# A linear-attention layer and a gated convolution unit: keys and values two tokens to a row, 64-row matmul tiles, a compact state and a new order of the work

## The chip, the cores and the metric

The kernel runs on one core of a Trainium2 chip. The core has a matrix engine (TensorE, PE in the profile; its weight loads are PEld), a vector engine (VectorE, DVE), a scalar engine (ScalarE, ACT), a general one (GpSimd, POOL) and a queue engine (SyncE, SP) that mostly issues DMAs. The matrix engine writes its results into PSUM, eight banks of 512 fp32 columns on 128 partitions; VectorE and ScalarE read them from there. The engines run side by side and wait for one another by semaphores. The metric is the device time of one execution in microseconds, here the median of several runs.

## The reference

Inputs are r, k and v of shape (4 batches, 8 heads, 768 tokens, 48 channels), decays w and bonuses u of shape (8, 48), and three weights of the second layer. All are fp32.

```python
state = zeros((B, H, D, D))
for t in range(S):
    cur = einsum('bhd,bhe->bhde', u * k[t], v[t])
    y[t] = einsum('bhd,bhde->bhe', r[t], state + cur)
    state = w[:, :, None] * state + einsum('bhd,bhe->bhde', k[t], v[t])
x = y.transpose(0, 2, 1, 3).reshape(B, S, H * D)        # 384 channels
gate = sigmoid(sum(conv_w[i] * shifted(x, 4 - i) for i in range(5)))   # causal, per channel
out = (gate * (x @ w_val)) @ w_out
```

The recurrence need not be run token by token. Within a chunk, y is a masked product of scores (r times k, with the decays folded into both) and v, plus r times the state at the chunk's start, plus the bonus of the token itself.

## The kernel before, in words

A unit is 256 tokens of one batch; there are 12 units, three to a batch, and each has two chunks of 128 tokens. For each unit the stages are, by the names of the order that is written out in the code:

- **r, k, v** load the inputs. r comes with two neighbouring tokens of a head to a partition row (`load_r`, 384 bytes in a piece), k and v with one token to a row (`load_kv`, 192 bytes in a piece), a chunk at a time.
- **RS, KS** multiply r and k by tables of decays (`scale_r` L245, `scale_k` L274; POOL, some on DVE). **RT, KT** transpose them on PE, eight 128x128 transposes each (L259, L297). **RE, KE** copy the transposes from PSUM on ACT (`evac_r` L267, which also brings r's two tokens of a row back into the order of time, and `evac_k` L307). **CV** casts v to bf16 (L283, ACT).
- **PR, S, SE, DV** make the bonus: r times k (L316, DVE), a sum over channels by matmuls with two columns (L328), its copy (L340), and v times it (L343, POOL).
- **A** makes the scores of a chunk, eight matmuls with 48 rows and 128 columns into two banks (L357); **M** masks one bank of them on DVE (L370), four to a unit.
- **KV, ID, ZE** keep the state. A matmul for two heads at a time gives a 96x96 block of which only the two 48x48 blocks on the diagonal count (L384); DVE adds the old state in PSUM (L396) and multiplies by a mask of 384 columns that also holds the decay (L401).
- **YD, Y** put y together in a bank for each chunk: the bonus by six matmuls with the identity (L412), the state's and the scores' part by matmuls of 128 rows and 32 columns (`mm`, L426), 28 to a chunk. **YE** copies it to xT, channels on partitions (L455, ACT).
- **C, SG, V, HT, O, OE, st** are the second layer: the convolution as matmuls with diagonal 64x64 blocks (`conv` L470, 40 to a unit), the sigmoid (L483, ACT), the value matmuls (L490 and L499), their product with the gate (L512, DVE), the projection (L522), its copy (L534, ACT) and the store. The last unit is done a chunk at a time (`conv_l`, `value_l` and so on).

Nothing plans this at run time. The string `ORDER` (L639) lists all stages of all units, and each engine gets its instructions in that order; `r:1*` with a star means the other queue or engine. So an instruction that waits holds back all that follows it on its engine. SP issues nearly all DMAs in that order too. The matrix engine's banks come from a pool of eight that hands out the next one (`bank`, L58).

Ahead of the units stand the tables: w is loaded, its log taken (LN), and four exponentials give the decays (DRI, DKI). `dummy` (D, L146) is three matmuls of 512 columns that compute nothing.

Of the kernel before, what the change touches and what calls it, by code (L numbers as in the profile page):

```python
# [12 lines left out]
AX = mybir.AxisListType  # L13
# [3 lines left out]
def kernel(  # L17
# [21 lines left out]
    U = 2  # L39
    W = U * C  # L40
    NU = S // W
    N = B * NU
# [3 lines left out]
    ld = ctx.enter_context(tc.tile_pool(name="ld", bufs=7))  # L46
    ldr = ctx.enter_context(tc.tile_pool(name="ldr", bufs=6))
    wk = ctx.enter_context(tc.tile_pool(name="wk", bufs=2))
    atp = ctx.enter_context(tc.tile_pool(name="atp", bufs=4))
    ffn = ctx.enter_context(tc.tile_pool(name="ffn", bufs=2))  # L50
    outp = ctx.enter_context(tc.tile_pool(name="outp", bufs=11))

    psum = ctx.enter_context(tc.tile_pool(name="psum", bufs=8, space=bass.MemoryType.PSUM))
# [4 lines left out]
    def bank(shape=(128, 512), dtype=F32):  # L58
        return psum.tile(list(shape), dtype, name="bank")

    k_st, v_st, r_st = {}, {}, {}

    def load_kv(n, cl, nm, eng):
        b, cu = divmod(n, NU)
        src, d = (k, k_st) if nm == "k" else (v, v_st)
        if n not in d:
            d[n] = ld.tile([128, U, H, D], F32, name=f"{nm}_st")
        t0 = cu * W + cl * C
        eng.dma_start(out=d[n][:, cl], in_=src[b, :, t0 : t0 + C, :].transpose([1, 0, 2]))

    def load_r(n, eng, hs=(0, H)):
        b, cu = divmod(n, NU)
        if n not in r_st:
            r_st[n] = ldr.tile([128, H, 2, D], F32, name="r_st")
        hs = slice(*hs)
        eng.dma_start(
            out=r_st[n][:, hs].rearrange("p h s d -> p h (s d)"),
            in_=r[b, hs, cu * W : cu * W + W, :].rearrange("h (p s) d -> p h (s d)", s=2),
        )

    w_bc = consts.tile([128, H, D], F32)
    cw5 = consts.tile([KW, DM], F32)

    def load_w():
        nc.sync.dma_start(
            out=w_bc.rearrange("p h d -> p (h d)"),
            in_=w.rearrange("(o h) d -> o (h d)", o=1).to_broadcast([128, DM]),
        )

    def load_cw():  # L90
        nc.sync.dma_start(out=cw5, in_=moe_conv_w)
# [3 lines left out]
    wt = consts.tile([128, NP], F32)  # L95
    nc.vector.memset(wt, 1.0)
    ut = consts.tile([128, NP], F32)
    nc.vector.memset(ut, 0.0)
    nc.scalar.preload_act_table_set("natural_log_exp_and_others")
    for dst, src in ((wt, w), (ut, u)):  # L100
        for par in range(2):
            nc.scalar.dma_start(
                out=dst[64 * par : 64 * par + D, :],
                in_=src.rearrange("(p two) d -> two d p", two=2)[par],
            )


    io_i32 = consts.tile([128, 1], mybir.dt.int32)
    nc.gpsimd.iota(io_i32, pattern=[[0, 1]], base=0, channel_multiplier=1)
    io_j = consts.tile([128, 2], mybir.dt.int32)  # L110
    nc.gpsimd.iota(io_j, pattern=[[1, 2]], base=0, channel_multiplier=2)
    mask = consts.tile([128, 128], BF16)
    make_upper_triangular(nc, mask, val=1.0, diag=False)

    io_f = consts.tile([128, 1], F32)
    nc.vector.tensor_copy(io_f, io_i32)
    sc_k = consts.tile([128, U], F32)
    for cl in range(U):
        nc.vector.tensor_scalar(
            sc_k[:, cl : cl + 1], io_f, scalar1=-1.0, scalar2=float(C - 1 - cl * C),  # L120
            op0=ALU.mult, op1=ALU.add,
        )
    sc_r = consts.tile([128, 2], F32)
    nc.vector.tensor_copy(sc_r, io_j)
    nc.vector.tensor_scalar_add(sc_r, sc_r, float(-C))

    lnw_bc = consts.tile([128, H, D], F32)
    dk = consts.tile([128, U, H, D], F32)
# [5 lines left out]
    def decay_r():  # L134
        for j in range(2):
            nc.scalar.activation(
                out=dr[:, :, j, :], in_=lnw_bc, func=AF.Exp, scale=sc_r[:, j : j + 1]
            )

    def decay_k():  # L140
        for cl in range(U):
            nc.scalar.activation(
                out=dk[:, cl], in_=lnw_bc, func=AF.Exp, scale=sc_k[:, cl : cl + 1]
            )

    def dummy():  # L146
        t_ = bank()
        for _ in range(3):
            nc.tensor.matmul(
                out=t_.rearrange("p (a x) -> p a x", x=128),  # L150
                lhsT=ident,
                rhs=ident[:, None, :].to_broadcast([128, 4, 128]),
                start=True,
                stop=True,
            )
# [3 lines left out]

    def heads(t_, n):  # L160

        return t_[:, 16 : 16 + 64 * n].rearrange("p (h x) -> p h x", x=64)[:, :, 0:D]
# [4 lines left out]
    ks_t = ring("ks", [128, U, NP, 2, 64], 3)  # L167
    rs_t = ring("rs", [128, 2, NP, 2, 64], 2)
    vb_t = ring("vb", [128, U, H * 64 + 64], 4)
    dv_t = ring("dv", [128, U, DM], 2)  # L170
    xT_t = ring("xT", [128, NT, PAD + S], 2)
    for t_ in rs_t:
        nc.gpsimd.memset(t_[:, :, :, :, D:64].rearrange("p s n a x -> p (s n a) x"), 0.0)
    for t_ in ks_t:
        nc.gpsimd.memset(t_[:, :, :, :, D:64].rearrange("p c n a x -> p (c n a) x"), 0.0)
    for t_ in vb_t:
        nc.gpsimd.memset(gaps(t_.rearrange("p c x -> p (c x)")), 0.0)
    for t_ in xT_t:
        nc.gpsimd.memset(t_[:, :, 0:PAD], 0.0)

    uw2 = consts.tile([128, NP, 2], BF16)
    nc.gpsimd.memset(uw2, 0.0)
    wcm = consts.tile([128, NP, 2, D], F32)
    nc.gpsimd.memset(wcm, 0.0)
    bdm = consts.tile([128, NP, 2, D], F32)
    nc.gpsimd.memset(bdm, 0.0)
    for par in range(2):
        nc.gpsimd.memset(bdm[64 * par : 64 * par + 64, :, par, :], 1.0)

    wv_st = consts.tile([128, NT, DM], F32)
    wo_st = consts.tile([128, NT, DM], F32)

    wval = consts.tile([128, NT, 4, 128], BF16)
    wout = consts.tile([128, 4, DM], BF16)
    cw5b = consts.tile([KW, DM], BF16)
    cwT = consts.tile([128, NT, KW], F32)
    cwd = consts.tile([128, NT, KW, 64], BF16)
    id64 = consts.tile([128, 64], BF16)  # L200

    for q in range(2):
        rows = slice(64 * q, 64 * q + 64)
        nc.vector.tensor_copy(id64[rows], ident[rows, rows])
# [4 lines left out]
    def cw_transp():  # L209
        st["cw_ps"] = bank([128, NT, 8], BF16)  # L210
        for T in range(NT):
            nc.tensor.transpose(
                st["cw_ps"][:, T, 0:KW], cw5b[:, T * 128 : T * 128 + 128], ident[0:KW, 0:KW]
            )
# [4 lines left out]
    def cw_diag():  # L219
        nc.vector.tensor_tensor(  # L220
            out=cwd.rearrange("p t k x -> p (t k) x"),
            in0=id64[:, None, :].to_broadcast([128, NT * KW, 64]),
            in1=cwT.rearrange("p t k -> p (t k)")[:, :, None].to_broadcast([128, NT * KW, 64]),
# [3 lines left out]
    def cast_wval():  # L227
        wv = wv_st.rearrange("p k (t x) -> p k t x", x=128)
        nc.gpsimd.tensor_copy(wval[:, :, 0::2, :], wv[:, :, 0::2, :])
        nc.gpsimd.tensor_copy(wval[:, :, 1::2, 64:128], wv[:, :, 1:3, 0:64])  # L230
        nc.gpsimd.tensor_copy(wval[:, :, 1::2, 0:64], wv[:, :, 1:3, 64:128])

    def cast_wout(part):
        if part:
            nc.scalar.copy(out=wout[64:128, 1::2, :], in_=wo_st[0:64, 1:3, :])
            nc.scalar.copy(out=wout[0:64, 1::2, :], in_=wo_st[64:128, 1:3, :])
        else:
            nc.gpsimd.tensor_copy(wout[:, 0::2, :], wo_st[:, 0::2, :])


    st = {}

    def scale_r(n, eng, ps=(0, NP)):
        hs = slice(2 * ps[0], 2 * ps[1])
        eng.tensor_tensor(  # L245
            out=rs_t[n % 2][:, :, ps[0] : ps[1], :, 0:D].rearrange("p s n a d -> p (n a) s d"),
            in0=r_st[n][:, hs],
            in1=dr[:, hs],
            op=ALU.mult,
        )  # L250

    def transp_r(n, ps=(0, NP)):
        if ("rT", n) not in st:
            st["rT", n] = wk.tile([128, NP, W], BF16, name="rT", bufs=3)
        q = ps[1] - ps[0]
        tr = bank([128, 2, q, 128], BF16)
        for p in range(q):
            for s in range(2):
                nc.tensor.transpose(  # L259
                    tr[:, s, p, :],  # L260
                    rs_t[n % 2][:, s, ps[0] + p].rearrange("p a x -> p (a x)"),
                    ident,
                )
        st["r_tr", n, ps[0]] = tr

    def evac_r(n, ps=(0, NP)):
        nc.scalar.copy(  # L267
            out=st["rT", n][:, ps[0] : ps[1], :].rearrange("x n (i s) -> x s n i", s=2),
            in_=st["r_tr", n, ps[0]],
        )  # L270

    def scale_k(n, eng, cls=(0, U)):
        cs = slice(*cls)
        eng.tensor_tensor(  # L274
            out=ks_t[n % 3][:, cs, :, :, 0:D].rearrange("p c n a d -> p c (n a) d"),
            in0=k_st[n][:, cs],
            in1=dk[:, cs],
            op=ALU.mult,
        )

    def cast_v(n):
        vb = vb_t[n % 4]
# [531 lines left out]
```

## Time and profile before

| what | value |
|---|---|
| median of 3 runs | 104.22 us (103.72 to 104.8) |
| profiled execution: span from first to last instruction | 102.6 us |
| PE, DVE, ACT, POOL busy in it | 84.6, 75.7, 72.8, 58.2 us |
| DMA | 20.55 MB in 67,645 packets, 63,525 of them under 512 bytes |
| matmuls; mean granted clock of the matrix engine | 2,016; 0.944 |

The median is 1.6 us above the span; that part lies around the first and last instruction. "Busy" counts an engine as busy where an instruction of it runs; matmuls overlap and their ends are modelled. L-numbers are lines of the kernel before. In rows of groups, `xN | busy, mean` are the count, the summed time in us and the mean of one in ns, followed by the idle time just before and what ended it.

### The profile page before, as it was taken

How to read it: one execution, taken by the hardware profiler on the slowest of the kernel's cores; microseconds unless marked ns; L12 is line 12 of the kernel's file. 1: busy time of each engine (PE TensorE's matmuls, PEld its weight loads, DVE VectorE, ACT ScalarE, POOL GpSimd, SP SyncE). 2: the span in 40 equal slices, each digit the busy share in tenths (PEclk: the TensorE clock that was granted, in tenths of full speed). 3: DMA queues.
4: the chain of work that ended last, by engine and by line, in shares of the span. 5: the costliest groups of instructions: out<-in, count | busy, mean ns of one | idle time of the engine just before them, and what ended most of it. 6: DMA issues, size and time to landing. Idle time of an engine off the chain costs nothing.

```text
span 102.6 us, 4615 instructions
## 1 busy us (share of the span) xinstructions
PE 84.6 (82%) x2016; PEld 68.3 (67%) x2016; DVE 75.7 (74%) x148; ACT 72.8 (71%) x123; POOL 58.2 (57%) x63
## 2 busy tenths in 40 slices
PE   0002846999987999999899979999899999999980
PEld 0002435878766887898687648997698978887830
DVE  4004465886999998998789499999875986997230
ACT  5056555941988799977969967988798499835840
POOL 7951049799683706983995678738166990140000
PEclk9999996555899999999999999999999999999997
DMA  1799999999888799697979799879899897088673
GB/s 35 145 246 245 207 166 183 237 224 318 151 257 155 150 234 201 125 240 151 255 134 244 151 194 279 163 152 257 123 200 162 163 356 262 6 296 312 233 273 126
DMA packets 67645, 20.55 MB, mean 200 GB/s; under 512 B 63525, under 2 KB 67626, under 8 KB 67626
## 3 DMA queue, kind: packets, MB, share of 16 engines
q1 hardware_dynamic: 65610, 19.77, 86.8%
q10 hardware_dynamic: 2016, 0.49, 2.4%
q8 instruction: 15, 0.25, 1.0%
q14 instruction: 4, 0.03, 0.1%
HBM read 15.54 MB, written 4.72 MB: 198 GB/s over the span
## 4 chain that ended last, share of the span: by engine, by line
PE 51%; DMA 16%; DVE 13%; ACT 8%; issue 4%; POOL 3%; SPq 2%; DVEq 0%; POOLq 0%; ACTq 0%
PE bank L470 8%; PE bank L522 7%; PE bank L426 6%; DMA r_st<-in_r_dram 6%; DMA k_st<-in_k_dram 6%; PE bank L490 5%; DVE at L370 5%; DMA cw<-in_moe_conv_w_dram 5%; PE bank L297 5%; ACT kT L307 4%; PE bank L357 4%; PE bank L259 4%; PE bank L499 3%; PE bank L412 2%; PE bank L384 2%
## 5 line engine op out<-in xcount | busy, mean ns | idle before, releaser
L370 DVE TENSOR_TENSOR at<-bank,mask 128x512 bf16<-128x512 f32 x48 | 31.2, 681 | 3.3 <-PE bank L357 2.9
L343 POOL TENSOR_TENSOR dv<-v_st,s_sb 128x768 bf16<-128x768 f32 x12 | 17.7, 1475 | 12.5 <-DVE s_sb L340 10.9
L274 POOL TENSOR_TENSOR ks<-k_st,dk 128x768 bf16<-128x768 f32 x9 | 16.7, 1859 | 11.8 <-DVE cw5b L207 5.4
L307 ACT COPY kT<-bank 128x1024 bf16<-128x1024 bf16 (+1 forms) x13 | 12.4, 956 | 9.3 <-DVE pr L316 6.4
L267 ACT COPY rT<-bank 128x1024 bf16<-128x1024 bf16 (+1 forms) x13 | 16.1, 1237 | 2.5 <-PE bank L259 2.2
L259 PE MATMUL bank<-ident,rs 128*128 128x128 bf16 x96 | 8.4, 234 | 10.5 <-DVE rs L245 9.7
L245 POOL TENSOR_TENSOR rs<-r_st,dr 128x768 bf16<-128x768 f32 x8 | 14.5, 1818 | 3.0 <-DMA r_st<-in_r_dram 3.0
L522 PE MATMUL bank<-wout,hT 128*128 128x384 bf16 x66 | 14.2, 326 | 0.1
L259 PEld LDWEIGHTS <-rs 128*128 128x128 bf16 x96 | 6.3, 104 | 11.7 <-POOL uw L689 9.7
L455 ACT CAST xT<-bank 128x384 bf16<-128x384 f32 x24 | 10.7, 488 | 4.5 <-PE bank L426 4.4
L512 DVE TENSOR_TENSOR hT<-bank,gate 128x384 bf16<-128x384 f32 x22 | 11.6, 546 | 0.2 <-PE bank L522 0.2
L483 ACT ACTIVATE gate<-bank 128x384 bf16<-128x384 f32 x22 | 9.8, 500 | 2.6 <-PE bank L470 1.8
L470 PE MATMUL bank<-xT,cwd 64*64 64x128 bf16 (+1 forms) x440 | 11.2, 244 | 0.6 <-DVE at L370 0.3
L534 ACT COPY o_sb<-bank 128x384 f32<-128x384 f32 x22 | 10.3, 488 | 1.4 <-PE bank L522 0.9
L470 PEld LDWEIGHTS <-cwd 64*64 64x64 bf16 x440 | 9.7, 106 | 1.9 <-issue 0.8
L490 PE MATMUL bank<-xT,wval 128*128 128x256 bf16 x66 | 10.8, 272 | 0.0
L297 PE MATMUL bank<-ident,ks 128*128 128x128 bf16 x96 | 8.6, 239 | 2.4 <-DVE ks L274 1.4
L316 DVE TENSOR_TENSOR pr<-bank,rT 128x1024 bf16<-128x1024 bf16 (+1 forms) x13 | 8.3, 642 | 3.0 <-ACT kT L307 1.7
L283 ACT CAST vb<-v_st 128x768 bf16<-128x768 f32 x12 | 10.2, 852 | 0.0
L426 PE MATMUL bank<-at,vb 128*32 128x128 bf16 x384 | 9.8, 230 | 0.0
L357 PE MATMUL bank<-rT,kT 48*128 48x128 bf16 x192 | 8.8, 229 | 0.7 <-DVE bank L396 0.3
L297 PEld LDWEIGHTS <-ks 128*128 128x128 bf16 x96 | 6.6, 107 | 4.2 <-DVE ks L274 2.2
(79 smaller groups left out, 140.1 us busy)
## 6 DMA issues: line engine op xcount, KB each, us to landing
k_st<-in_k_dram SPq DMA_DIRECT2D x24, 192.0 KB, 5.4
v_st<-in_v_dram SPq DMA_DIRECT2D x24, 192.0 KB, 4.8
out_dram<-o_sb SPq DMA_DIRECT2D x11, 384.0 KB, 4.5
r_st<-in_r_dram SPq DMA_DIRECT2D x10, 384.0 KB, 5.4
wv_st<-in_moe_w_val_dram SPq DMA_DIRECT2D x1, 576.0 KB, 6.5
wo_st<-in_moe_w_out_dram SPq DMA_DIRECT2D x1, 576.0 KB, 6.3
r_st<-in_r_dram SPq DMA_DIRECT2D x2, 192.0 KB, 5.5
r_st<-in_r_dram ACTq DMA_DIRECT2D x1, 384.0 KB, 5.5
```

The lines of the kernel that those rows point to most:

```text
L245: eng.tensor_tensor(out=rs_t[n % 2][:, :, ps[0] : ps[1], :, 0:D].rearrange("p s n a d -> p (n a) s d"), in0=r_st[n][:, hs], in1=dr[:, hs], ...
L259: nc.tensor.transpose(tr[:, s, p, :], rs_t[n % 2][:, s, ps[0] + p].rearrange("p a x -> p (a x)"), ident,)
L267: nc.scalar.copy(out=st["rT", n][:, ps[0] : ps[1], :].rearrange("x n (i s) -> x s n i", s=2), in_=st["r_tr", n, ps[0]],)
L274: eng.tensor_tensor(out=ks_t[n % 3][:, cs, :, :, 0:D].rearrange("p c n a d -> p c (n a) d"), in0=k_st[n][:, cs], in1=dk[:, cs], op=ALU.mult,)
L297: nc.tensor.transpose(tr[:, c, p, :], ks[:, cls[0] + c, p].rearrange("p a x -> p (a x)"), ident,)
L307: nc.scalar.copy(out=st["kT", n].rearrange("x n (c i) -> x c n i", c=U)[:, cls[0] : cls[1]], in_=tr,)
L343: eng.tensor_tensor(out=dv_t[n % 2].rearrange("p c (h d) -> p (c h) d", d=D), in0=v_st[n].rearrange("p c h d -> p (c h) d"), in1=st["s", n ...
L370: nc.vector.tensor_tensor(out=st["at", n, cl][:, par], in0=st["at_ps", n, cl][par], in1=mask[:, None, :].to_broadcast([128, NP, 128]), op= ...
L426: nc.tensor.matmul(out=y_ps[32 * q : 32 * q + 32, T, :], lhsT=lt, rhs=rh, start=False, stop=last, skip_group_check=True,)
L470: nc.tensor.matmul(out=g_ps[i][64 * qo : 64 * qo + 64, o0 : o0 + n0], lhsT=cwd[rows, T, t, :], rhs=xT[rows, T, t0 + c0 + t : t0 + c0 + t + ...
L490: nc.tensor.matmul(out=v_ps[:, 0:W], lhsT=wval[:, kt, i, :], rhs=xT[:, kt, t0 : t0 + W], start=(kt == 0), stop=(kt == NT - 1), skip_group_ ...
L522: nc.tensor.matmul(out=o_ps, lhsT=hT[:, i, c0 : c0 + C], rhs=wout[:, k, :], start=(j == 0), stop=(j == 2),)
```

## The change

- **Loads.** k and v are loaded as r was, two tokens to a row, all eight heads of a unit in one DMA (`load_tok`; the first unit in halves of four heads). The decay table of k follows that layout. w and u for the state and the bonus come as rows and are transposed on PE (WUT, WUE). The value and output weights are cast for a rotation of channels by 32 in place of 64.
- **Tokens.** In a unit, partition q holds tokens 2q and 2q + 1 (s = 0, 1), so a chunk is 64 rows and two tokens. r's copy from PSUM no longer brings the order of time back.
- **Scores, state, y.** All use tiles of 64 rows. `attn` makes 16 matmuls with 64x64 tiles for each key token s and puts both chunks into one pair of banks. `state` makes 32 matmuls with 64 rows and 48 columns and leaves only the diagonal blocks, 192 columns. The state is then kept in that compact form by F, Z1, G and ZN (three on DVE, one on ACT). y takes its parts by YX and YZ (state), YD (bonus) and Y (scores) with 64x32 tiles, and writes them through `y_view`, which steps over every second column of the bank, so that y is in the order of time there.
- **Convolution.** Diagonal blocks of 32x32, 60 matmuls of 256 columns to a unit into three banks, three sigmoids in place of two.
- **Banks.** Eight banks are fixed; each stage of the order names those that it uses (`A:0.0/45`). Most intermediate tiles are fixed rings too. Output tiles are 8 in place of 11.
- **Order and engines.** The order is written anew, with eight groups of dummies (`D:4/1` is four matmuls into bank 1), memsets on DVE, and some stages on other engines: a star is DVE or the ACT queue, a plus is POOL or, for elementwise stages, ACT.

```diff
-    def load_kv(n, cl, nm, eng):
...
-        eng.dma_start(out=d[n][:, cl], in_=src[b, :, t0 : t0 + C, :].transpose([1, 0, 2]))
+    def load_tok(n, nm, src, eng, hs):
...
         eng.dma_start(
+            out=st[nm, n][:, hs].rearrange("p h s d -> p h (s d)"),
+            in_=src[b, hs, cu * W : cu * W + W, :].rearrange("h (p s) d -> p h (s d)", s=2),
         )
...
+    BANK = [psum.tile([128, 512], F32, name=f"bank{i}") for i in range(8)]
...
+    def evac_r(n, eng, ps=(0, NP)):
+        a = slice(*ps)
+        cp = eng.copy if eng is nc.scalar else eng.tensor_copy
+        cp(out=rT_t[n % NRT][:, :, a], in_=st["r_tr", n][:, :, a])
...
+    def attn(n, sk, bs):
...
+        for p in range(NP):
+            for h in range(2):
+                for par in range(2):
+                    rows = slice(64 * par, 64 * par + D)
+                    q = slice(64 * h, 64 * h + 64)
+                    nc.tensor.matmul(
+                        out=at_ps[par][q, p, :],
+                        lhsT=kT[rows, sk, p, q],
+                        rhs=rT[rows, :, p, q],
...
+    def state(n, bs):
...
+        for s in range(2):
+            for p in range(NP):
+                for par in range(2):
+                    for h in range(len(bs)):
+                        q = slice(64 * h, 64 * h + 64)
+                        nc.tensor.matmul(
+                            out=kv[h][64 * par : 64 * par + 64, p, :],
+                            lhsT=ks[q, s, p, par, :],
+                            rhs=heads(vb[q, s], H)[:, 2 * p + par, :],
...
+    def carry0(n):
+            nc.vector.tensor_tensor(
+                out=f_t[n % 2], in0=st["X", n], in1=heads(zn_t[n % 2], NP), op=ALU.add
+            )
+    def carry1(n):
+        nc.vector.tensor_tensor(out=f_t[n % 2], in0=st["Y", n], in1=f_t[n % 2], op=ALU.add)
+    def z_next(n):
+        nc.vector.tensor_tensor(
+            out=heads(zn_t[(n + 1) % 2], NP),
+            in0=f_t[n % 2],
+            in1=wct[:, :, None].to_broadcast([128, NP, D]),
+            op=ALU.mult,
+        )
+    def y_view(n, c):
+        return st["y", n, c].rearrange("x t (q s) -> x t s q", s=2)
...
+    PIECES = [
+        [(p, x, 3 * p + (1 if x else 2 * par), ((16, 32), (48, 0))[x][par])
+         for x in range(2) for p in range(NP)]
+        for par in range(2)
+    ]
+    def y_bonus(n, bs):
+        for G in range(3 * NP):
+            for s in range(2):
+                for h in range(2):
+                    q = slice(64 * h, 64 * h + 64)
+                    ymm(n, h, G, dv[q, s, 32 * G : 32 * G + 32], ident[q, q], s)
+    def y_attn(n, sk, bs):
+        for i in range(2 * NP):
+            for par in range(2):
+                p, x, G, c0 = PIECES[par][i]
+                for h in range(2):
+                    q = slice(64 * h, 64 * h + 64)
+                    e = 64 * (2 * p + par) + c0
+                    ymm(
+                        n, h, G, vb[q, sk, e : e + 32],
+                        at[q, sk, par, p, :].rearrange("p (s q) -> p s q", s=2),
+                    )
...
+    def conv(n, cl, bs):
+        for t in range(KW):
+            for q in range(4):
+                for T in range(NT):
+                    rows = slice(32 * q, 32 * q + 32)
+                    qo = (q + T) % 4
+                    nc.tensor.matmul(
+                        out=bank(bs[T])[32 * qo : 32 * qo + 32, 0:wd],
+                        lhsT=cwd[rows, T, t, :],
+                        rhs=xT[rows, T, t0 + t : t0 + t + wd],
...
-        WCT k:0.0 w r:1 r:0.1 k:1.0 r:0.0 LN DRI k:0.1 k:1.1 cw DKI WCM r:2* UW RSP:0.1 KS:1 v:0.1
-        RS:1* RSP:0.0 KSP:0.0 KSP:0.1 RTP:0.1 D:11 REP:0.1 RTP:0.0 KTP:0.0 REP:0.0 KEP:0.0 v:0.0
...
+        ZZ:2* r:0.1 w wu* cw r:0.0 ZZ:1* MK LN D:4/1 WUT/0 DR:1 k:0.0 WUE ZZ:0* DR:0 CWB RS:0.0*
+        r:1 DK:0 DK:1 ID KS:0.0* k:0.1 RS:0.1* D:9/2 KT:0.0/1 RT:0.1/2 KE:0.0* RT:0.0/2 KS:0.1*
+        k:1 RE:0.1 RE:0.0 CWT/3 UW D:1/4 KT:0.1/1 RS:1 KE:0.1* PR:0 D:2/6 A:0.0/45 k:2 KS:1 WCT
+        KS:2 RT:1/6 A:0.1/70 RE:1 v:0 r:2 D:3/1 KT:1/2 RS:2 M:0.0 KE:1 S:0/1 M:0.3 D:3/6
+        A:1.0/40 v:1 M:0.2 CWC v:2 SE:0 CWD DV:0 PR:1 CV:0 TL D:1/3 Y:0.1/67 M:1.0 KV:0/31
...
+        A:4.1/50 KT:5/2 KS:6 M:4.2 r:7 KV:4/34 F:4 YE:3.1 C:3/617 M:4.3 O:2.1/5 KE:5 SG:3.0
+        V:3.1/3 PR:5 SG:3.1 Z1:4 G:4 V:3.0/0 YX:4/61 SG:3.2 OE:2.1 RS:6 HT:3.1 A:4.0/27 A:5.1/45
...
+        OE:10.1* VL:11.3/0 OL:11.0/5 GL:11.3 GL:11.5 st:8 HL:11.2 HL:11.3 XL:11.0 OL:11.2/6
+        XL:11.2 st:9 OL:11.1/2 st:10 stl:11.0 stl:11.2* XL:11.1* stl:11.1
```

## The prediction

> **What bounds the kernel now.** I read the page's busy times first, then the same by stage, then the chain that ended last for what each TensorE stage takes, then the first 16 us of the timeline.
>
> The head of the page: busy time by engine, and the clock and DMA rows in 40 slices of 2.57 us.
> ```profile
> span 102.6 us, 4615 instructions
> ...
> PE 84.6 (82%) x2016; PEld 68.3 (67%) x2016; DVE 75.7 (74%) x148; ACT 72.8 (71%) x123; POOL 58.2 (57%) x63
> ...
> PEclk9999996555899999999999999999999999999997
> DMA  1799999999888799697979799879899897088673
> ```
> Over the whole span no engine looks full. By stage (columns: stretch, its length, busy us and instructions of each engine, granted clock, DMA share):
> ```profile
> 0.00:10.00 10.00, 0.27 (x3) 0.30 (x4) 2.12 (x11) 4.23 (x8) 6.21 (x30) 1.00 0.78 166
> 10.00:16.00 6.00, 3.69 (x34) 2.21 (x32) 3.68 (x8) 3.60 (x5) 1.65 (x1) 1.00 1.21 188
> 16.00:26.30 10.30, 10.08 (x171) 8.14 (x171) 7.62 (x17) 5.43 (x8) 8.43 (x6) 0.50 1.14 243
> ...
> 40.00:64.00 24.00, 22.86 (x556) 18.25 (x557) 20.70 (x40) 19.93 (x35) 18.91 (x12) 1.00 0.96 196
> 64.00:88.00 24.00, 23.52 (x606) 20.09 (x598) 20.31 (x38) 20.26 (x34) 13.99 (x9) 1.00 0.89 198
> ```
> Two regimes. From 26 us on PE is busy 95 to 98% of the time, with DVE and ACT about 85% right behind. Before that the kernel only fills: 10 us without PE work, 6 us with little, then 10.3 us in which PE is busy but at half clock.
>
> The chain gives what a stage costs when PE goes through it without a wait (start, us, matmuls):
> ```profile
> 63.83 1.78 PE bank L470 x80
> 65.61 0.55 PE bank L297 x8
> 66.16 0.17 PE bank L384 x4
> ...
> 74.66 0.90 PE bank L426 x56
> ...
> 79.31 0.45 PE bank L297 x8
> ...
> 95.67 1.00 PE bank L560 x80
> ```
> L297 is the same eight transposes twice: 0.45 us behind 128x128 matmuls, 0.55 us behind the 64x64 convolution. So **a change of the array's tile shape costs 0.10 us**. L426 (y, tiles of 128 rows x 32 columns): 0.90 less one change is 0.80 us for 14 groups of four tiles, so a group of 128 moving columns takes 0.057 us whether it is one matmul or four at once. L560: 0.90 us for ten groups of 128 and ten of 64 columns, 0.57 + 0.33, so a group of 64 costs 0.033. L470: 1.68 for ten groups of 256 and ten of 128, so 0.111 for 256.
>
> **PE, part by part.** "Unit" is 256 tokens; there are 12. Before, us per unit: transposes of r and k 0.45 each, bonus sums S 0.2 (L328), scores A eight groups 0.45, state KV 8 x 0.042 = 0.34, YD 6 x 0.056 = 0.34, Y 14 groups 0.80, convolution 0.84, values 1.0, projections 0.98: 5.85, times 12 = 70.2, less 1.4 for the state work missing at batch ends = 68.8. The order written out has 60 changes of tile shape: 6.0. Together 74.8.
>
> After: transposes, S, values (two of 0.33 + 0.17) and projections (two of 0.49) as they are (3.08). Scores: 32 matmuls of 64x64, four at once, again eight groups: 0.45. KV: eight groups of 48 columns at the 0.033 of 64: 0.26. State part of y (YX, YZ): 32 matmuls, eight tiles at once, four groups: 0.23. YD: 48 matmuls of 64 columns; the two tokens of a row go to one tile one behind the other, so 12 pairs at 0.033 + 0.003 issue gap, about 0.40; bounds 0.20 (eight at once) and 0.79 (no overlap between pairs). Y: 64 matmuls; in half of them the eight tiles are distinct (0.11 for each key token), in the middle pieces (x=1) the two heads of a pair use the same tile in turn, four times two groups with a little for issue, 0.25: 0.36 twice, 0.72; bounds 0.46 (always eight at once) and 0.91 (never over four). Convolution: 60 matmuls of 32x32, twelve tiles at once, five groups of 256: 0.56; if never over four at once, 1.67. Sum 5.70, times 12 = 68.4. But the new order has 82 changes of shape, which I counted through it: 8.2. **Together 76.6: PE gets 1.8 us more, not less**; what the convolution saves, the changes of shape, YD and the doubled tiles of Y give back. Besides come 25 dummy matmuls of 512 columns; 13 stand ahead of the first transpose, where PE was idle anyway, 12 in the flow, 12 x 0.217 = 2.6 us, nearly all in waits of the start-up; I put 0.5 on the path, together with the store buffers (8 for 12 outputs, so the last evacuations wait for stores that take 4.5 us to land; 5 us of PE work lie between).
>
> [...]
>
> The second open thing is the output of y: its tokens now lie two to a row, so YX, YZ, Y and YD write every second fp32 column of their bank. No matmul before writes so. Nearest rows: a 128-column group into adjacent columns 0.057, a 256-column group, which covers as much of a bank, 0.111. Bounds: nothing, or double. Doubled: Y 1.10 twice against 0.36 twice, YD 1.36 against 0.40, state part 0.45 against 0.23, so +2.7 a unit, +32 us, all on PE. I take nothing, since the columns that move through the array stay 128, which is the nearer row; the other end makes the slow rival. [...]
>
> **DVE.** The 48 masks stay (681 ns each, 31 us). Out: 20 state products (550 ns) and 8 carries (558), 15.5. In: 28 on 192 elements, at the 352 ns of L599's 192: 9.8. Half the convolution diagonal, -0.8. Scales of r and k moved away, about -3.7; five full and two half evacuations that come here at about the 642 of the product L316, +4.0; three output copies +1.5. Net -4.5 of 75.7. The memsets that come to its start, about 3 us, fit ahead of the first scale, at 9.03 now.
>
> **ACT.** These rows bear on it:
> ```profile
> L307 ACT COPY kT<-bank 128x1024 bf16<-128x1024 bf16 (+1 forms) x13 | 12.4, 956 | 9.3 <-DVE pr L316 6.4
> L267 ACT COPY rT<-bank 128x1024 bf16<-128x1024 bf16 (+1 forms) x13 | 16.1, 1237 | 2.5 <-PE bank L259 2.2
> ```
> The r copy loses its interleaved write, and three go to DVE: -6.7. k copies -3.2, casts of v to POOL -3.4, output copies -1.4. In: three gates of 256 in place of two of 384 (between 331 and 500 ns, 0.38): +3.9 with the last unit; the state copies 12 x 0.33 = +3.9; weight casts +0.7. Net -6. POOL about +2, with 40 us free.
>
> **DMA.** The trace's packets of 192 B take 17.4 ns in the mean, those of 384 B 24.8. 49,152 of the first become 24,576 of the second: 855 us of engine time become 609, or 15 us less on each of 16 engines that are 87% busy. SP issues k and v in one go per unit in place of two.
>
> **The start.** DVE's first scale waits for r until 9.03; the first mask stands at 15.46:
> ```profile
> 9.03 2.11 DVE L245 TENSOR_TENSOR rs<-r_st,dr 128x384 bf16<-128x384 f32 x3 [6.45 <-DMA r_st<-in_r_dram]
> ...
> 10.11 1.49 PE L149 MATMUL bank<-ident 128*128 128x512 bf16 x3
> ...
> 15.46 1.29 DVE L370 TENSOR_TENSOR at<-bank,mask 128x512 bf16<-128x512 f32 x2
> ```
> k:0.0, w and the whole of r:1 are issued ahead of the half of r that the first scale needs; now that half goes first and w second. By packet times r:0.1, w, r:0.0 and k:0.0 need 0.8 + 0.6 + 0.8 + 0.8 = 3 us; with the 2.5 us to the first bytes and 0.5 of tail w is there at about 5 to 6 instead of 6.1. Log and two exponentials (0.5 + 0.6 + 0.6) put the first scale at about 7. Then on DVE: k's two exponentials on ACT until 8.4, three half scales, two half evacuations, one product to about 12.1, which is 3.4 us earlier than 15.46. Bounds 1.5 and 5.
>
> The clock: three dummies took 1.49 us where 512 columns at full clock cost 0.217 each, so PE was cold there too (the clock row begins only after that), warm to 16, cold to 26.3. At half clock 10.3 us of work cost 5.1; the chain runs over PE for some 8 of these 10.3, so at most 4.1 is on the path. 13 dummies, 13 x 0.43 = 5.6 us of cold work from about 1.6 us on, and 12 more in the gaps hold PE busier than the 3.7 of 6 us after which it fell back. I take -3.5; bounds 0 and -5.1.
>
> **The sum,** against the profiled span: 102.6 - 3.4 (start) - 3.5 (clock) - 2.0 (of PE's 2.7 us idle from 26.3 to 88, with DVE, ACT and DMA relieved) + 1.8 (PE work) + 0.5 = 96.0. The median of the runs is 104.22, 1.6 above the span of the profiled execution, which covers what lies around it. **Forecast 97.6 us.** With the better bounds of start, clock and Y it is about 91.5.
>
> **Rivals.** *Strided writes of y* (slower): +32 us if double, 129.6. It decides from 1.2 times the contiguous time on, where it eats the 6.6 us gained. For: nothing in the trace writes so; against: every group's time here follows its moving columns. 0.17. *No more than four tiles at once*: convolution +1.11, Y +0.38, state part +0.23 a unit, +20.6: about 118. For: the trace shows four at most; against: four cost no more than one. 0.06. *The start gives nothing* (PE falls to half clock again, or w lands no sooner): 104.2 less 2.0 plus 2.3, about 104.5. 0.11. *The written-out banks make waits*: the pool took any free bank of eight, now each stage names its own; PE has no slack for it; 0.4 us a unit and more leads to 103 to 108. 0.05. The forecast keeps 0.61.
>
> A measurement of this kernel can tell about 1% from no change. Faster by over 1%: the forecast and part of the third, 0.66; within 1%: 0.08; slower: 0.26. The range goes from 91.5 to 114; outside lie strides worse than 1.5 times, most of the four-tile case and a little below, 0.17.
>
> **What will show it.** Right: first mask near 12 us, clock up from 10 us on, L-lines of the convolution at 0.56 + 0.10 in the chain, Y at 0.3 to 0.45, DMA share under 0.8, DVE about 71 plus memsets. Wrong: Y stages of 0.7 us or more (stride), convolution over 1 us (tiles), a clock row with fives up to 26 us, or PE idle in the steady part behind evacuations.

## The result, and the profile after

The changed kernel takes **141.78 us** (median of 4 runs, 140.86 to 145.1) against 104.51 of the kernel before beside it, a ratio of **1.359 (95% interval 1.347 to 1.370)**. The forecast was 97.6, its range ended at 114, and the slow rivals stood at 103 to 129.6: it is slower than all of them. Some executions of these kernels run a little long at the same work; medians below include such runs, so the fastest run stands beside them, while ratios leave them out, and the profiled executions of experiments 3, 4, 7 and 8 are among the long ones (2 to 4% above the fastest of their kernel).

The page of the changed kernel (span 139.1 us in an execution of 140.86): head, busy times, rows in slices of 3.48 us, DMA queues, and the shares of the chain that ended last.
```profile
span 139.1 us, 8027 instructions
...
PE 104.1 (75%) x3700; PEld 75.9 (55%) x3700; DVE 76.2 (55%) x172; ACT 65.6 (47%) x138; POOL 62.1 (45%) x52
...
PEclk9999999757999999968999999999999995999999
DMA  3999998999999999998410000000000770012053
...
q8 instruction: 28, 0.46, 1.3%
...
PE 70%; issue 19%; DVE 4%; DMA 2%; ACT 2%; POOL 0%; ACTq 0%; POOLq 0%; DVEq 0%
```
The same queue and chain lines of the page before:
```profile
q8 instruction: 15, 0.25, 1.0%
...
PE 51%; DMA 16%; DVE 13%; ACT 8%; issue 4%; POOL 3%; SPq 2%; DVEq 0%; POOLq 0%; ACTq 0%
```
Two things stand out. 3,700 matmuls with 3,700 weight loads have taken the place of 2,016 and 2,016. And 19% of the chain, 26 us, is "issue": time in which PE waited for nothing that the profile shows. Before, that share was 4%.

The stretches of the kernel after, in the columns of the table in the prediction:
```profile
16.00:26.30 10.30, 7.30 (x335) 5.16 (x334) 6.40 (x15) 5.78 (x12) 9.34 (x8) 0.99 1.02 257
...
40.00:64.00 24.00, 16.96 (x611) 12.56 (x611) 11.76 (x25) 9.97 (x21) 14.11 (x9) 0.93 1.07 249
64.00:88.00 24.00, 18.68 (x804) 14.71 (x802) 15.14 (x31) 13.18 (x26) 10.69 (x7) 1.00 0.17 56
```
No engine is full any more: PE fell from 23.5 of 24 us to 18.7, and DVE and ACT with it. From 70 us on the loads are over (DMA share 0.17 over 64 to 88 us), so it isn't the loads alone either. The chain from 68 to 83 us (start, us, matmuls) shows where the time goes:
```profile
68.90 0.59 PE bank L558 x3
69.49 0.75 PE bank L502 x60
70.25 0.28 PE bank L329 x8
70.53 0.25 PE bank L290 x4
70.78 1.45 issue
72.23 0.38 PE bank L290 x4
72.62 0.35 PE bank L358 x16
...
77.25 0.30 PE bank L385 x24
77.56 1.58 issue
79.14 0.25 PE bank L385 x8
...
81.61 1.54 issue
```
PE stops in the middle of a stage (L290 after four of its eight transposes, L385 after 24 of 32 matmuls), for about 1.5 us, although the rest of the stage needs nothing new.

The place of these stops is regular. I counted PE's instructions in the trace, matmuls, weight loads and eight others, by their start. Of the 21 pauses of over 0.6 us, 17 come after 704, 960, 1216, 1728 and so on, always 192 plus a multiple of 256. The page gives the reason to look there: the queue "q8 instruction" moved 0.25 MB before and 0.46 MB after, about 62 bytes for each PE instruction, in packets of 16 KB, so one packet is about the 256 instructions between the stops. From this I read theory F: **PE comes to the end of a block and waits for the instructions of the next one**. Measured are only the counts and the packets' times. The times agree with it if the first packet of a kernel holds what follows instruction 448, as I take it: in the changed kernel the second one moved from 21.55 to 22.78 us, and PE, which had stopped at 21.60 behind 704, went on at 24.14. In the eight kernels here that stop (table in experiment 6), PE goes on 1.2 to 1.8 us after the block's packet has landed, at each of their 90 stops. Where the packet had landed more than 1.1 us before PE came to the block, there is none; in the kernel before, the shortest such lead is 1.5 us.

What became of the time, from the start of one matmul to the start of the next (us, profiled executions):

| | before | after |
|---|---|---|
| steps up to 0.6 us, summed (of them dummies) | 85.9 (1.3) | 98.5 (7.3) |
| steps over 0.6 us | 3.6 (3 steps) | 35.8 (21 steps; 17 at ends of blocks, 31.2) |
| ahead of the first and after the last matmul | 13.1 | 4.8 |
| span | 102.6 | 139.1 |

So +36.5 us is 32.2 of stops and 12.6 of matmul time, less 8.3 at the ends (dummies now fill the front). Of the 12.6, dummies are 6.0 and the parts of y 9.1 (17.3 to 26.4 us); all else together got 2.6 shorter.

### The profile page after: what moved, and what is told of

Read it like the earlier page. It is cut to its first block, busy times and chain, and to the rows that moved or that the text cites. A ratio compares the mean times of both kernels' runs of the same rounds, so it can differ in the third digit from the quotient of the medians.

```text
span 139.1 us, 8027 instructions
## 1 busy us (share of the span) xinstructions
PE 104.1 (75%) x3700; PEld 75.9 (55%) x3700; DVE 76.2 (55%) x172; ACT 65.6 (47%) x138; POOL 62.1 (45%) x52
## 2 busy tenths in 40 slices
DMA packets 41972, 20.77 MB, mean 149 GB/s; under 512 B 37837, under 2 KB 41938, under 8 KB 41938
## 4 chain that ended last, share of the span: by engine, by line
PE 70%; issue 19%; DVE 4%; DMA 2%; ACT 2%; POOL 0%; ACTq 0%; POOLq 0%; DVEq 0%
PE bank L430 20%; PE bank L532 10%; PE bank L558 8%; PE bank L290 8%; PE bank L502 8%; PE bank L358 6%; PE bank L153 4%; PE bank L385 2%; DMA wu<-in_u_dram 2%; PE bank L329 2%; DVE at L370 1%; ACT kT L309 1%; PE bank L570 1%; ACT rT L304 1%; DVE zn L410 1%
## 5 line engine op out<-in xcount | busy, mean ns | idle before, releaser
L343 POOL TENSOR_TENSOR dv<-v_st,s 128x768 bf16<-128x768 f32 x12 | 19.0, 1586 | 39.3 <-DVE s L340 18.3
L430 PE MATMUL bank<-at,vb 64*32 64x128 bf16 x768 | 17.6, 317 | 4.6 <-issue 4.0
L278 POOL TENSOR_TENSOR ks<-k_st,dk 128x768 bf16<-128x768 f32 x11 | 19.8, 1810 | 1.1 <-DMA k_st<-in_k_dram 1.1
L532 PE MATMUL bank<-xT,wval 128*128 128x128 bf16 (+2 forms) x156 | 16.8, 257 | 1.6 <-issue 0.9
L518 ACT ACTIVATE gt<-bank 128x256 bf16<-128x256 f32 (+1 forms) x26 | 9.1, 369 | 18.1 <-PE bank L502 18.1
L545 DVE TENSOR_TENSOR hT<-bank,gt 128x384 bf16<-128x384 f32 (+1 forms) x26 | 13.0, 521 | 8.1 <-PE bank L532 3.4
L358 PE MATMUL bank<-rT,kT 48*64 48x128 bf16 x384 | 11.1, 236 | 7.4 <-issue 7.2
L502 PE MATMUL bank<-xT,cwd 32*32 32x256 bf16 (+1 forms) x780 | 11.3, 273 | 5.4 <-issue 5.4
L532 PEld LDWEIGHTS <-wval 128*128 128x128 bf16 x156 | 12.9, 103 | 4.3 <-issue 2.0
L430 PEld LDWEIGHTS <-vb 64*32 64x32 bf16 x768 | 10.7, 111 | 6.7 <-issue 5.8
L430 PE MATMUL bank<-ident,dv 64*32 64x64 bf16 x576 | 10.3, 244 | 2.9 <-issue 2.7
```

The costliest lines, as they stand in the source:

```text
L278: eng.tensor_tensor(out=tok_major(ring_[n % len(ring_)][:, :, ps[0] : ps[1], :, 0:D]), in0=st[nm, n][:, hs], in1=tab[:, hs], op=ALU.mult,)
L343: eng.tensor_tensor(out=dv_t[n % NDV].rearrange("p s (h d) -> p h s d", d=D), in0=st["v", n], in1=s_t[n % 2].rearrange("p s h -> p h s")[: ...
L358: nc.tensor.matmul(out=at_ps[par][q, p, :], lhsT=kT[rows, sk, p, q], rhs=rT[rows, :, p, q], start=(p == 0), stop=(p == NP - 1), skip_group ...
L430: nc.tensor.matmul(out=y if s is None else y[:, s, :], lhsT=lt, rhs=rh, start=fresh, stop=False, skip_group_check=True,)
L502: nc.tensor.matmul(out=bank(bs[T])[32 * qo : 32 * qo + 32, 0:wd], lhsT=cwd[rows, T, t, :], rhs=xT[rows, T, t0 + t : t0 + t + wd], start=(t ...
L532: nc.tensor.matmul(out=v_ps[:, o0 : o0 + n0], lhsT=wval[:, kt, T, :], rhs=xT[:, kt, t0 + c0 : t0 + c0 + n0], start=(o0 == 0 and kt == 0), ...
```

## The experiments

F, my reading of the stops: the supply of instructions holds PE back, by blocks of 256. Rivals: S, the strided writes of y (the slow rival of the prediction), and A, the time that the matmul groups need in the array.

**1. y into adjacent columns.** ACT's copy (shown at 3) puts the two tokens in order, not PE's write.
```diff
     def y_view(n, c):
-        return st["y", n, c].rearrange("x t (q s) -> x t s q", s=2)
+        return st["y", n, c].rearrange("x t (s q) -> x t s q", s=2)
```


> Theory S (strided writes): the changed kernel's y groups take about 0.109 us where a contiguous group of 128 columns takes 0.057; with contiguous writes (the copy out of PSUM does the interleaving instead) 24 Y stages, 24 state stages and 12 bonus stages lose half of their time, some 1.3 us a unit, and the time falls from 141.8 to about 126. Theory F (instruction supply): the matrix engine gets its instructions in blocks of 256, a block takes 3.4 us or more to come, and 17 stops at multiples of 256 instructions make 31 us; the number of instructions stays 7,400, so what y saves is mostly spent waiting for the next block: 135 to 140.

Measured: 144.63 us (143.66 to 145.06), ratio 1.390 (1.382 to 1.399): not faster, but about 2% slower than the changed kernel. The stride does cost array time; Y's row on the page of the changed kernel and, below it, of this one:
```profile
L430 PE MATMUL bank<-at,vb 64*32 64x128 bf16 x768 | 17.6, 317 | 4.6 <-issue 4.0
```
```profile
L430 PE MATMUL bank<-at,vb 64*32 64x128 bf16 x768 | 12.7, 240 | 4.4 <-issue 4.3
```
317 ns a matmul became 240, yet the whole gained nothing: 16 stops with 30.5 us were left of 17 with 31.2. y's steps fell by 6.5 us (26.4 to 19.9), and all other matmul steps rose by 7.7, at a mean granted clock of 0.864 against 0.950. S doesn't explain the 36 us. F's 135 to 140 was missed too: it held for the stops and left out the clock. Experiment 6 comes back to it.

**2. The bonus part of y by 12 matmuls in place of 48.** Same columns moved, same stride, 864 PE instructions fewer.
```diff
-        for G in range(3 * NP):
+        for T in range(NT):
...
-                    ymm(n, h, G, dv[q, s, 32 * G : 32 * G + 32], ident[q, q], s)
+                    nc.tensor.matmul(
+                        out=y_view(n, h)[:, T, s, :],
+                        lhsT=dv[q, s, 128 * T : 128 * T + 128],
+                        rhs=ident[q, q],
```


> The bonus part of y by 12 matmuls of 64 rows and 128 columns in place of 48 of 64x32; its writes stay strided and the array time stays the same (6 pairs of 64 strided columns, 0.32 us either way). Theory F: 864 instructions fewer, 3.4 blocks at 3.7 to 4.9 us, so 12 to 16 us less: 126 to 130. Theory S: nothing changes, 140 to 143.

Measured: 128.8 us (127.76 to 130.54), ratio 1.236 (1.226 to 1.246): 13 us less for 864 instructions, 15 ns each, while the array's own work is hardly changed. F's number, not S's. "issue" falls to 13% of its chain.

**3. Both:** the edits of 1 and 2 together, with ACT's copy of 1, which both need:
```diff
-        nc.scalar.copy(out=xT_t[b % 2][:, :, t0 : t0 + C], in_=st["y", n, c])
+        nc.scalar.copy(
+            out=xT_t[b % 2][:, :, t0 : t0 + C].rearrange("x t (q s) -> x t q s", s=2),
+            in_=st["y", n, c].rearrange("x t (s q) -> x t q s", s=2),
+        )
```


> Both edits together. Theory F alone: as the second run, 126 to 130. Theory S alone: as the first, 126. Both true: each block of 256 instructions now also needs less array time, but cannot come faster than 3.4 to 5 us; 25.5 blocks at 4.2 us and 15 us of start give about 120; range 112 to 127.

Measured: 128.45 us (125.65 to 129.86): little from the stride again, 2 us by the fastest runs, and nearer to F alone (126 to 130) than to the 120 of both together.

**4. The kernel before with more instructions.** Its scores, its y and its convolution are each done in two halves of their columns: the same columns, loads and order (y's bonus part stays whole), 6,544 PE instructions in place of 4,032.
```diff
-            for t in range(KW):
+            for t, j in ((t, j) for t in range(KW) for j in range(2)):
...
+                        n0 //= 2
+                        c0, o0 = c0 + j * n0, o0 + j * n0
```


> The kernel before, with every matmul of the scores, of y and of the convolution split in two of half the columns: same work and contiguous writes, but 6,544 instructions of the matrix engine in place of 4,032. By array time alone (a pair of half groups costs 0.009 us more than one whole group) 3 us more: 107.5. Theory F: 25.6 blocks at 4.2 to 4.9 us from 15 us on: 120 to 135, with stops of the matrix engine at multiples of 256 instructions that the kernel before does not have.

Measured: 136.82 us (133.11 to 138.79), about 30 us slower than the kernel that it was made from, with the same marks in the chain:
```profile
55.86 0.45 PE bank L259 x8
56.30 0.33 PE bank L496 x3
56.63 1.87 issue
58.50 0.34 PE bank L505 x3
...
65.11 0.94 PE bank L476 x71
66.06 2.35 issue
68.41 0.28 PE bank L476 x9
```
The convolution stops after 71 of 80 matmuls. Stops at ends of blocks: 13, 23.4 us; the kernel before has none. Another 12.1 us are matmul steps (85.9 to 98.0), at a granted clock of 0.875 against 0.944; how much of that is the clock isn't shown. More instructions alone, without anything else of the change, cost nearly as much as the change.

**5. The rates by themselves.** Two kernels that compute none of the outputs. The first runs ten groups each of whole and of 64x32 tiles, into adjacent and into every second column, and then 2,048 small matmuls of 64 columns that wait for nothing; the second runs 4,096 of these while all loads of r, k and v run, laid out as in the changed kernel.
```python
for g in range(groups):
    for q in range(4):
        for h in range(2):      # eight tiles, 64 columns
            nc.tensor.matmul(out=BANK[b0 + h][32 * q : 32 * q + 32, 0:64],
                             lhsT=a[64 * h : 64 * h + 64, 32 * q : 32 * q + 32], ...)
```


> No part of the reference is computed; zeros are stored. The matrix engine alone runs, without a wait: ten groups of eight 64x32 tiles with 256 columns, contiguous and then to every second column; ten whole 128x128 matmuls with 256 columns both ways; ten groups of eight with 128 columns both ways; then 256 groups of eight 64x32 tiles with 64 columns. Theory S: a contiguous group 0.111 and 0.057 us, a strided one double, for whole matmuls as for tiles. Theory F: the last part, 4,096 instructions, takes 16 blocks at 3.4 us or more, 54 us and up, with stops at multiples of 256; by array time (0.033 a group) it would take 8.5 us.

> Computes none of the outputs, zeros are stored: 36 dummies of 512 columns and then 4,096 matmuls of 64x32 tiles with 64 columns (8,192 PE instructions, nothing to wait for), while the 36 loads of r, k and v, two tokens to a row, run from the start on as in the changed kernel. Without loads the same stream took 3.45 to 3.73 us for 256 instructions. Theory F with loads in the way: 4.3 to 5.3 us for 256 instructions while the loads run, 3.4 to 3.8 after. Loads without influence: 3.4 to 3.8 throughout. Time with influence about 130 to 150 us, without about 115 to 125.

Measured, rates: the two rows below hold ten groups into adjacent and ten into every second column each.
```profile
16.05 3.41 PE L82 MATMUL bank<-a 128*128 128x256 bf16 x20
19.39 1.97 PE L72 MATMUL bank<-a 64*32 64x128 bf16 x160
```
From start to start a 128x128 matmul of 256 columns takes 0.109 us into adjacent columns and 0.216 into every second one. Eight 64x32 tiles of 128 columns take 0.056 together in the quickest groups and 0.067 in most, and 0.109 with the stride; with 256 columns, in the first 6.4 us of the run, it is 0.213 and 0.427. **In all three the stride doubles the array's time.** Measured, supply: timeline rows of PE in the second kernel (span 133.4 us, time 135.21), first under the loads, then after them:
```profile
26.76 1.28 PE L72 MATMUL bank<-a 64*32 64x64 bf16 x128 [3.82 <-issue]
30.76 1.27 PE L72 MATMUL bank<-a 64*32 64x64 bf16 x128 [2.73 <-issue]
35.04 1.27 PE L72 MATMUL bank<-a 64*32 64x64 bf16 x128 [3.00 <-issue]
...
81.53 1.28 PE L72 MATMUL bank<-a 64*32 64x64 bf16 x128 [2.18 <-issue]
84.99 1.27 PE L72 MATMUL bank<-a 64*32 64x64 bf16 x128 [2.18 <-issue]
88.72 1.27 PE L72 MATMUL bank<-a 64*32 64x64 bf16 x128 [2.45 <-issue]
```
128 matmuls and their 128 loads are done in 1.27 us (the granted clock of the whole run was 0.577 in the mean), and then PE stands for 2.2 to 3.8 us. A block comes every 3.59 us in the mean when nothing else moves (16 blocks, 71.95 to 129.41 us) and every 4.56 us under the loads (11 blocks, 18.07 to 68.22): 14 and 18 ns for each instruction. The stream waits for no semaphore, so these stops are not data. By these periods the 28.9 blocks of the changed kernel need 104 to 132 us of supply; the 15.8 of the kernel before need 57 to 72, which its 85.9 us of PE's steps cover.

**6. Fewer instructions in the convolution too.** On top of experiment 2, and with y into adjacent columns on top of 3, the convolution as 30 matmuls with 64x64 blocks.
```diff
-            for q in range(4):
-                for T in range(NT):
-                    rows = slice(32 * q, 32 * q + 32)
-                    qo = (q + T) % 4
+            for T in range(NT):
+                for q in range(2):
+                    rows = slice(64 * q, 64 * q + 64)
+                    qo = (q + T) % 2
```


> The changed kernel with two parts made of fewer and larger matmuls: the bonus part of y as 12 matmuls of 64x128 in place of 48 of 64x32, and the convolution as 30 matmuls on 64x64 tiles in place of 60 on 32x32 tiles. PE executes 5,816 instructions instead of 7,400; the convolution needs the array longer (ten groups of 256 columns, 1.11 us, in place of five, 0.56: +6.6 us over 12 units). y still writes every second column. Theory F (the supply of instructions holds PE back): from the changed kernel to the one with 12 bonus matmuls 864 instructions fewer took 13.0 us off, 15.0 ns each; another 720 fewer take 10.8 us off 128.8: about 118 us (115 to 122). Theory A (PE is held by the time its groups need in the array): +6.6 us, about 135.

> The same with y written into adjacent columns of its banks (ACT's copy reorders the two tokens of a row instead). Theory F alone: like the run with strided y, 118 us, since the number of instructions is the same. Theory F with the stride behind it: with 5,816 instructions there is room for the array's time to show, and the run is faster than the strided one by 5 to 12 us: 106 to 113. Neither expects it clearly below the kernel before (104): it still executes 5,816 instructions against 4,032.

Measured: 123.91 us (122.14 to 125.43) with the stride and 123.14 (122.17 to 128.74), ratio 1.184 (1.173 to 1.194), without it. The first lies between F (118) and A (135): by the fastest runs 5.6 us less than experiment 2 for 780 instructions fewer (the last unit's convolution is done in two parts), where F gave 10.8. Between the profiled executions (126.6 and 121.1 us) the stops fell by 7.5 us, and the convolution's matmul steps grew from 11.0 to 14.7. So here this 3.7 came on top of what the supply set; the longer one didn't hide the other. I read it so: PE stops only where small matmuls follow one another faster than a block every 3.6 to 4.6 us, and elsewhere its stages take their own time.

The second missed the 106 to 113 that I gave it. y's steps did fall, 25.2 to 17.4 us, 7.7 less. But all matmul steps together fell only 3.6 us (100.4 to 96.8): convolution, values and projections took 4.2 us more. And pauses over 0.6 us rose from 15.2 to 19.8. The same convolution in the chain, first with the stride, then without:
```profile
58.49 1.47 issue
59.96 0.32 PE bank L358 x9
60.28 0.59 PE bank L569 x3
60.88 1.21 PE bank L513 x30
```
```profile
59.92 1.95 issue
61.87 0.32 PE bank L358 x9
62.20 1.06 PE bank L572 x3
63.26 2.27 PE bank L516 x18
```
After the longer stop PE runs at about half speed (1.06 for 0.59), and the granted clock over 40 to 64 us is 0.86 against 1.00. So the gain was taken back by longer pauses and by stretches of slower clock. That a stop drops the clock is argued from such places, not tested by itself, and a stop alone doesn't decide it: in the kernel with the stride two stops of 2.2 and 2.0 us (at 27.4 and 37.9 us) passed with the clock at 1.00 until the end of the work. In the profiled executions of all three pairs the kernel without the stride had the lower mean clock (0.864 against 0.950, 0.878 against 0.987, 0.951 against 0.998); why is open.

The stops against the number of PE instructions, for all kernels (profiled executions):

| kernel | PE instructions | stops at ends of blocks | their sum, us | span, us |
|---|---|---|---|---|
| before | 4,032 | 0 | 0 | 102.6 |
| before, loads (7) | 4,032 | 0 | 0 | 102.6 |
| before, loads and dummies (8) | 4,092 | 4 | 4.3 | 105.9 |
| 2 + 64x64 convolution, adjacent | 5,756 | 9 | 12.1 | 121.9 |
| 2 + 64x64 convolution | 5,756 | 7 | 10.0 | 121.1 |
| bonus by 12 (2) | 6,536 | 11 | 17.5 | 126.6 |
| bonus by 12, adjacent (3) | 6,536 | 13 | 19.8 | 128.1 |
| before in halves (4) | 6,544 | 13 | 23.4 | 136.3 |
| after | 7,400 | 17 | 31.2 | 139.1 |
| after, adjacent (1) | 7,400 | 16 | 30.5 | 141.8 |

**7. The start, in the kernel before.** The head of the order is rearranged: the half of r that the first scale needs is loaded first, then w, much as in the changed kernel. The state's decay (WCT) moves behind the tables of decays, and the second unit's scale of r (`RS:1*`) behind the first unit's scales.
```diff
-        WCT k:0.0 w r:1 r:0.1 k:1.0 r:0.0 LN DRI k:0.1 k:1.1 cw DKI WCM r:2* UW RSP:0.1 KS:1 v:0.1
-        RS:1* RSP:0.0 KSP:0.0 KSP:0.1 RTP:0.1 D:11 REP:0.1 RTP:0.0 KTP:0.0 REP:0.0 KEP:0.0 v:0.0
+        r:0.1 w k:0.0 cw r:0.0 k:0.1 LN DRI r:1 k:1.0 k:1.1 DKI WCT WCM r:2* UW RSP:0.1 KS:1 v:0.1
+        RSP:0.0 KSP:0.0 KSP:0.1 RS:1* RTP:0.1 D:11 REP:0.1 RTP:0.0 KTP:0.0 REP:0.0 KEP:0.0 v:0.0
```


> The kernel before with the head of its order alone changed: the half of r that the first scale needs is loaded first, then w, and the state's decay is computed behind the tables of decays, no longer ahead of them. By the prediction's start term the first mask comes 1.5 to 3.4 us sooner and the time falls by about as much, to 101 to 103. Rival: the matrix engine is at half clock from 16 to 26 us whatever comes first, and the time stays within 1 us of 104.5.

Measured: 104.55 us (102.03 to 105.84) against 104.78, ratio 0.988 (0.976 to 0.999): about 1%, hardly clear of noise (the interval ends just short of 1), where 101 to 103 us were expected. It is the only kernel here that isn't slower than the one before. Its chain:
```profile
12.10 0.35 PE bank L357 x8
...
12.54 1.30 DVE at L370 x2
...
13.87 1.78 POOL ks L274
...
15.70 1.03 PE bank L297 x8
```
and the same place before:
```profile
14.38 1.79 POOL ks L274
...
16.22 1.04 PE bank L297 x8
```
The first mask came 2.9 us earlier (12.54 for 15.46), but PE then stood 3.3 us for the second unit's k, which POOL scaled from 13.87 on, only 0.5 us earlier. The second half of that k landed at 13.7; the profile names the masks, which ended at 13.8, as the release. Which of the two it was is open.

**8. The same with early dummies,** 22 matmuls at the start and 11 in gaps of the first stages in place of 3, to hold the clock (a number behind `D:` now counts matmuls). Against the kernel of 7, two of the four lines that change:
```diff
-        r:0.1 w k:0.0 cw r:0.0 k:0.1 LN DRI r:1 k:1.0 k:1.1 DKI WCT WCM r:2* UW RSP:0.1 KS:1 v:0.1
+        D:22 r:0.1 w k:0.0 cw r:0.0 k:0.1 LN DRI r:1 k:1.0 k:1.1 DKI WCT WCM r:2* UW RSP:0.1 KS:1 v:0.1
-        RSP:0.0 KSP:0.0 KSP:0.1 RS:1* RTP:0.1 D:11 REP:0.1 RTP:0.0 KTP:0.0 REP:0.0 KEP:0.0 v:0.0
+        RSP:0.0 KSP:0.0 KSP:0.1 RS:1* RTP:0.1 D:3 REP:0.1 RTP:0.0 KTP:0.0 REP:0.0 KEP:0.0 v:0.0
...
```


> As the run before, with 22 dummy matmuls of 512 columns ahead of the first transpose and 8 in the gaps of the first stages. By the prediction's clock term the matrix engine stays at full clock from about 6 us on, and 2 to 4 us more go: 98 to 101. Rival: the dummies stand in front of real work and the gain of the clock is given back: 102 to 104.

Measured: 107.35 us (104.6 to 109.57). The clock was up until 24 us (0.982 in the mean of the profiled execution, 0.967 in experiment 7), and nothing was gained. Against experiment 7 the matmuls other than dummies took 4.5 us less (83.8 to 79.3), but the dummies took 8.6 more (1.3 to 9.9). And stops now appear at ends of blocks (4.3 us, the third row of the table), one of them behind the convolution:
```profile
76.06 1.81 PE bank L470 x80
77.86 0.11 PE bank L328
77.97 1.54 issue
79.52 0.31 PE bank L328 x7
```
By theory F the kernel before is close to such stops in places: the shortest lead of a packet over PE is 1.5 us. With 60 instructions more, all in the first stages, the ends of blocks fall elsewhere in the work, and at four of them the lead is 1.0 us or less.

## Why the prediction was wrong, step by step

- **PE's sum is the step that failed:** "a group of 128 moving columns takes 0.057 us whether it is one matmul or four at once", and the 76.6 us built on it. As array time it holds (eight tiles took 0.056 in the quickest groups). How closely matmuls can start isn't the cause either: experiment 5 did 128 small ones in 1.27 us, 10 ns each. But I counted columns and changes of shape only and gave the number of instructions no price. The unit's 268 small matmuls stand in the sum by their columns alone; the packets of instructions behind them I never looked at, though the page's DMA part showed 15 before. In place of +1.8 us came 31.2 us of stops (experiments 2, 4 and 5). The terms of y were too small besides: its steps grew by 9.1 us where they gave +2.5, and the stride is most of that.
- **Strided writes taken at nothing: wrong as a rate.** They double a group (experiment 5: 0.056 us in the quickest groups to 0.109 for eight tiles of 128 columns). The rival's mechanism was right and its price, +32 us, too high: y's steps differ by 7.7 us (experiment 6), and the whole by nothing, since the time went into pauses and clock instead. The +32 isn't double the forecast's own terms either: those (0.72, 0.40 and 0.23) give 1.35 a unit, 16 us. The row that I called nearest, columns moved, was the wrong one; the row of the bank's width that I kept as the other end (0.111 for 256) was right.
- **Eight and twelve tiles at once: right.** The convolution took 0.75 us in the chain with its change of shape (0.56 + 0.10 forecast), Y without the stride 8.46 / 12 = 0.71 us a unit in the last kernel of experiment 6 (0.72). The rival of four tiles at most falls; its +0.38 for Y should have been 0.91 - 0.72 = 0.19, which makes it about 116 in place of 118.
- **Start -3.4: right for the mask, wrong as a gain.** First scale at 6.63 (7 forecast), first mask at 12.38 (12.1). The first packets of the loads start at 1.8 us before and 1.9 after, in place of the 2.5 that I put down, and w landed at 4.8 (5 to 6):
```profile
6.63 0.53 DVE L278 TENSOR_TENSOR rs<-r_st,dr 128x384 bf16<-128x384 f32 x1
...
12.38 0.68 DVE L370 TENSOR_TENSOR at<-bank,mask 128x512 bf16<-128x512 f32 x1
```
  By experiment 7 the mask was the wrong mark: there it came 2.9 us earlier, and PE then stood 3.3 us for the second unit's k, which POOL scaled only 0.5 us earlier.
- **Clock -3.5: wrong.** It was up as forecast (1.00 granted from 9.1 to 26.2 us), but experiment 8 gave up in dummies and stops what the clock saved, and the kernel before itself took 103.6 us in a run at a mean clock of 1.00 and 103.72 in one at 0.95. At that stage the chain hung on loads, POOL and DVE. Later the changed kernel had stretches of low clock of its own (0.75 over 26 to 40 us).
- **Dummies +0.5: too small.** 25 of them take 7.3 us of PE's steps. In the chain nine hold 3.6 us from 6.0 on, and the first transposes of k come behind them at 9.46, though k was scaled at 8.41; from 11 to 18 us others hold 2.1.
- **DVE, ACT, DMA: about right** and of no weight. DVE 76.2 (forecast 71 plus 3 of memsets), ACT 65.6 (66.8), POOL 62.1 (60.2), packets 67,645 to 41,972, loads over at 70 us. The 2.0 us of PE's idle time that their relief was to take away can't be seen: PE now has 17 stalls of another kind.
- **Written-out banks make waits:** not seen as a cause; in the chain of the changed kernel DVE and ACT hold 6%.

## What to carry to other kernels

Count PE's instructions, matmuls and weight loads together, beside the array's time: experiment 5 ran 256 of them every 3.6 us, 4.6 under full loads. By these periods, as my estimate, cutting matmuls into smaller tiles pays only as long as the whole stays above some 14 to 18 ns for each instruction. Look at the chain's "issue" share and at PE stopping in the middle of a stage, and at the packets of the instruction queue. A first step that comes earlier need not be a gain: in experiment 7 the first mask came 2.9 us earlier, what the next unit waited for 0.5, and the time fell by about 1%.

## What the runs showed that I had not expected

- The stops themselves, and that in experiment 6 they and array time added up: 3.59 us for 256 instructions quiet, 4.56 under loads, against 1.27 us to execute 256 small ones. In the changed kernel a packet of 16 KB took 0.9 to 1.7 us to move, and PE went on 1.2 to 1.6 us after it at the 17 stops. What makes up the rest of the period isn't shown.
- In experiment 5 a write into every second fp32 column of a bank took twice the array's time for whole and for small tiles (0.109 to 0.216 us, 0.056 in the quickest groups to 0.109).
- Less array time need not help a kernel that is short of instructions: without the stride, experiment 1 lost what y saved at a lower granted clock (0.864 against 0.950), and the last kernel of experiment 6 in longer pauses and at a lower clock (0.951 against 0.998).
